# Windowed attention and a SwiGLU block in one kernel: the queries of batch 1 turned by DMA, and all steps in another order

## The chip, the cores and the metric

The kernel runs on one core of a Trainium2 chip. The metric is the device time of one execution in microseconds (us). Engines: PE (TensorE), DVE (VectorE), ACT (ScalarE), POOL (GpSimd), SP (SyncE); SP, ACT and POOL also issue DMA transfers.

## The reference, cut to what matters

```python
q, k, v: (4, 8, 768, 64)            # batch, heads, sequence, head_dim
scores = q @ k.T / sqrt(64)
keep = (key < 8) | (0 <= query - key < 96)       # 8 global keys, a window of 96
scores = where(keep, scores - slope[h] * dist, -1e9)
a = exp(scores - max); a = a / (sum(a) + 1e-9)
x = (a @ v), heads side by side: (3072, 512)
g = x @ w_gate; out = (silu(g) * (x @ w_val)) @ w_out      # 512 -> 1536 -> 512
```

Inputs and output are float32; the kernel works in float16 with float32 sums in PSUM.

## The kernel before, in words

The kernel is one long list of steps, the string `ORDER`, read from left to right by a small interpreter at the end of the kernel. A step is a name and numbers (`g.2.11@4` is the gate product of token tile 2, feature block 11, into PSUM bank 4). Each step issues its instructions to one or more engines; every engine then runs its own instructions strictly in that order and waits only for data, for a buffer or for a bank. So where a step stands in the list sets what stands behind it on its engine. The steps are:

- Loads, all issued by POOL with a cast to float16: `Lh.i.half...` (half a sequence of keys, i=0, or queries, i=1, of some heads of batch 0, line 249), `L4.i.g` (four heads of batch 1 at once, 384 KB, line 287), `Lr.b.i.h` (one head of batch b in rows, 96 KB, line 292), `Lv`, `Lt`, `LG` (values, their tail, the global rows; lines 255, 261, 266), `Lw` (512 columns of the gate or value weights, line 299), `Lo` (output weights, line 307). A load waits until the eighth load before it has landed, since eight semaphores go round.
- Turning keys and queries so that the head dimension lies on partitions. Batch 0: `T` on PE (line 358), then `k` and `q` copies out of PSUM. Batch 1: `U` on PE (line 399), then `kw` (keys) and `qw` (queries, line 412). Batches 2 and 3: `D.b.hp.i`, a DMA transpose that SP issues (line 420) into `kN` (keys, i=0, three buffers) or straight into `qT` (queries, i=1, six buffers); `K.b.hp.e` (lines 427 to 430) spreads the keys `kN` into chunks, with its large copy on the engine e (V is DVE, A is ACT) and two small ones on DVE. hp is a pair of heads.
- Attention: `c.b.g.u` scores on PE (line 448), `x` their exp on ACT (457), `m` the mask on DVE (478), `w.b.half.what` the weighing on PE (505 for the sums, 511 for the values), `i`, `r` the inverse of the sums and its spreading on DVE (521 to 529), `p` the scaled result `xT` on DVE (540).
- The block behind it, for eight tiles of 384 tokens: `g` and `v` products on PE (553), `t` tanh on ACT (559), `s` and `h` the silu and the product on DVE (563, 570), `o.t.i.part` output products on PE (588; 585 for the last rows), `e.t.i` the output's copy on ACT into `osb` (two buffers, line 602) and its store by SP (603). The last rows, `e.7.2`, are copied in halves by ACT and DVE (597, 598) and stored by two queues (599, 600).
- `G` copies the global rows of values along (SP, 283); `fill.n` is n matmuls on ones into a bank that nobody reads (338); `M`, `Z`, `Y`, `VG`, `Gc`, `Li`, `Ld` prepare masks, zeros, first global rows and constants.

Tiles of a kind (`st`, `kN`, `qT`, `osb`, `xT`, ...) share a ring of buffers; a new tile takes the one that was given up first in the order of the program, and its first writer waits for that tile's last reader. `st`, into which keys and queries are loaded, has seven.

The lines that turn batch 1 on PE, and those that turn a batch by DMA:

```python
def tr_whole(bank, hp, i):
    ...
    for j in range(JW):                      # 8 by 2 transposes
        for hi in range(2):
            nc.tensor.transpose(
                t16[64 * hi:64 * hi + 64, PT * j:PT * j + PT],
                stage(1, i, hp // 2)[:, 2 * (hp % 2) + hi, D * j:D * j + D], ident)
...
def tr_dma(b, hp, i):
    ...
    nc.sync.dma_start_transpose(
        out=dst.rearrange("r (t p) -> r t p", t=J),
        in_=stage(b, i, hp // 2)[:, hp % 2].rearrange("p t e d -> p (t e d)"))
```

## Time and profile before

| what | value |
|---|---|
| median of three runs | 245.55 us (245.31 to 247.51) |
| the profiled execution: its time, its span | 247.71 us, 245.6 us |
| PE busy | 234.9 us, 96% of the span |
| DVE, ACT, POOL busy | 162.3, 105.4, 87.0 us |
| L399, transposes of batch 1 on PE | 128, 3.7 us busy |
| L358, transposes of batch 0 on PE | 128, 6.1 us busy |
| DMA queue of POOL, of SP: packets' time as a share of 16 engines' span | 65.2%, 18.5% |

The span runs from the first to the last instruction of the profiled execution; its own time is 2.1 us longer. Busy times of PE overlap, as a matmul starts before the one ahead of it has drained; the spacing of matmuls is read from the chain that ended last, which counts each stretch once. "PEclk" is the share of full clock speed granted to PE, "DMA share" the mean busy share of the 16 DMA engines, over 1 where transfers overlap on one.

### The profile page before, as it was taken

To read this page: it belongs to the slowest core of one execution; us is meant where nothing else is said; L and a number is where in the kernel's file an instruction comes from. 1 tells how busy PE (TensorE), PEld (TensorE's weight loads), DVE (VectorE), ACT (ScalarE), POOL (GpSimd) and SP (SyncE) were. 2 spreads that over 40 slices of the span, in tenths; PEclk is the share of its full clock that TensorE was granted. 3 is DMA by queue.
4 is the path that set the end of the run, shared out by engine and by line. 5 is a ranking of instruction groups with operands and counts; after the bars stand their busy time and mean duration, and the time that the engine had idled before them with its cause. 6 is when DMAs were issued, how large, how long until landed. Compare 5 with 4: busy or idle time off the path is not lost.

```text
span 245.6 us, 7237 instructions
## 1 busy us (share of the span) xinstructions
PE 234.9 (96%) x3112; PEld 137.3 (56%) x3112; DVE 162.3 (66%) x359; ACT 105.4 (43%) x191; POOL 87.0 (35%) x117
## 2 busy tenths in 40 slices
PE   8599999999999999999699999999999999999994
PEld 5376566664554555555355466545555655556643
DVE  5398998785275577837577769834898478505840
ACT  5495733745632533225573253235761142323321
POOL 8698695545999976980000000000000000000000
PEclk9858999999999999999999999999999999999999
DMA  7999999999999999999900374012000300021012
GB/s 103 161 160 161 179 141 178 206 195 91 173 173 144 180 137 160 120 159 200 115 3 0 120 168 42 0 45 88 3 0 15 121 0 3 0 85 43 3 42 86
DMA packets 82095, 24.57 MB, mean 100 GB/s; under 512 B 68896, under 2 KB 79120, under 8 KB 82064
## 3 DMA queue, kind: packets, MB, share of 16 engines
q0 software_dynamic: 64656, 14.20, 65.2%
q1 hardware_dynamic: 17224, 9.77, 18.5%
q8 instruction: 24, 0.39, 0.6%
q10 hardware_dynamic: 184, 0.14, 0.2%
q14 instruction: 7, 0.06, 0.1%
HBM read 28.51 MB, written 6.29 MB: 142 GB/s over the span
## 4 chain that ended last, share of the span: by engine, by line
PE 82%; DMA 9%; DVE 3%; POOL 2%; issue 1%; ACT 1%; ACTq 0%; POOLq 0%
PE PS L553 47%; PE PS L588 25%; PE PS L511 3%; DMA kN<-st 3%; DMA st<-in_q_dram 3%; DMA wv<-in_moe_w_val_dram 3%; PE PS L448 3%; PE PS L505 2%; PE PS L399 1%; PE PS L585 1%; POOL st L249 1%; DVE vS L277 1%; DVE qT L390 1%; ACT th L559 1%; DVE at L478 0%
## 5 line engine op out<-in xcount | busy, mean ns | idle before, releaser
L563 DVE SCALAR_TENSOR_TENSOR sl<-th,PS 128x384 f32<-128x384 f32 x96 | 50.8, 549 | 41.0 <-ACT th L559 40.4
L553 PE MATMUL PS<-xT,wg 128*128 128x384 f16 x384 | 72.6, 326 | 2.2 <-DVE hT L570 2.1
L553 PE MATMUL PS<-xT,wv 128*128 128x384 f16 x384 | 72.2, 326 | 0.1
L559 ACT ACTIVATE th<-PS 128x384 f32<-128x384 f32 x96 | 44.3, 491 | 59.0 <-PE PS L553 50.0
L588 PE MATMUL PS<-wo,hT 128*128 128x512 f16 x276 | 64.6, 379 | 0.0
L570 DVE TENSOR_TENSOR hT<-PS,sl 128x384 f16<-128x384 f32 x96 | 50.9, 552 | 10.4 <-PE PS L553 8.8
L553 PEld LDWEIGHTS <-wg 128*128 128x128 f16 x384 | 36.9, 98 | 28.2 <-issue 2.8
L553 PEld LDWEIGHTS <-wv 128*128 128x128 f16 x384 | 36.7, 98 | 25.6 <-DMA wv<-in_moe_w_val_dram 0.5
L588 PEld LDWEIGHTS <-hT 128*128 128x128 f16 x276 | 26.0, 98 | 28.7
L457 ACT ACTIVATE at<-PS 128x912 f16<-128x912 f32 (+1 forms) x40 | 31.6, 830 | 22.7 <-PE PS L448 22.6
L255 POOL DMA_DIRECT2D vS<-in_v_dram x40 | 33.2, 845 | 8.4 <-DMA wo<-in_moe_w_out_dram 3.0
L602 ACT ACTIVATE osb<-PS 128x512 f32<-128x512 f32 x23 | 13.7, 597 | 41.2 <-PE PS L588 41.2
L478 DVE TENSOR_TENSOR at<-at,masks 128x912 f16<-128x912 f16 (+5 forms) x56 | 22.5, 442 | 1.9 <-ACT at L457 1.9
L540 DVE TENSOR_TENSOR xT<-PS,rb 128x768 f16<-128x768 f32 x16 | 14.6, 952 | 7.2 <-PE PS L511 6.7
L292 POOL DMA_DIRECT2D st<-in_q_dram x16 | 14.4, 915 | 3.1 <-PE PS L553 1.4
L292 POOL DMA_DIRECT2D st<-in_k_dram x16 | 14.2, 912 | 0.5 <-DMA vS<-in_v_dram 0.5
L448 PE MATMUL PS<-qT,kT 64*64 64x152 f16 (+4 forms) x464 | 13.5, 238 | 0.5 <-DVE xT L540 0.4
L448 PEld LDWEIGHTS <-kT 64*64 64x64 f16 x464 | 8.6, 113 | 7.9 <-issue 6.8
L511 PE MATMUL PS<-at,vS 64*32 64x152 f16 (+4 forms) x1024 | 10.5, 218 | 0.4 <-issue 0.4
L511 PEld LDWEIGHTS <-vS 64*32 64x32 f16 x1024 | 9.3, 90 | 2.6 <-issue 2.3
L338 PE MATMUL PS<-ones 128*128 128x256 f16 x44 | 9.1, 387 | 1.2 <-DVE wg L304 1.2
L358 PE MATMUL PS<-ident,st 96*64 96x96 f16 x128 | 6.1, 268 | 3.0 <-DMA st<-in_k_dram 2.6
(50 smaller groups left out, 115.1 us busy)
## 6 DMA issues: line engine op xcount, KB each, us to landing
out_dram<-osb SPq DMA_DIRECT2D x23, 256.0 KB, 3.7
vS<-in_v_dram POOLq DMA_DIRECT2D x24, 91.0 KB, 5.6
wg<-in_moe_w_gate_dram POOLq DMA_DIRECT2D x6, 256.0 KB, 5.7
wv<-in_moe_w_val_dram POOLq DMA_DIRECT2D x6, 256.0 KB, 7.2
wo<-in_moe_w_out_dram POOLq DMA_DIRECT2D x3, 512.0 KB, 14.8
st<-in_q_dram POOLq DMA_DIRECT2D x16, 96.0 KB, 7.2
st<-in_k_dram POOLq DMA_DIRECT2D x16, 96.0 KB, 5.2
st<-in_q_dram POOLq DMA_DIRECT2D x4, 192.0 KB, 7.5
```

The source lines that it names most:

```text
L255: nc.gpsimd.dma_start(out=v_of(b)[CH * c + NG:CH * c + CH, c0:c1, j, :], in_=v[b, h, KC * c0:KC * c1, :].rearrange("(i p) d -> p i d", p=KC))
L292: nc.gpsimd.dma_start(out=stage(b, i, h % 2, True)[:, h // 4, :, h // 2 % 2, :], in_=KQ[i][b, h].rearrange("(t p) d -> p t d", p=128))
L448: nc.tensor.matmul(PS[64 * e:64 * e + 64, bank + hi, col:col + n], lhsT=kT_of(b, hp)[r, CH * c:CH * c + CH], rhs=qTs[b, hp][r, q0:q0 + n], ...
L457: nc.scalar.activation(out=at[:, :, 0:w], in_=PS[:, bank:bank + 2, 0:w], func=AF.Exp, scale=scale)
L478: ENG[e].tensor_mul(a2, a2, m2)
L511: nc.tensor.matmul(PS[r, bank + e, o:o + n], lhsT=V[s, c, j, what - 1::2], rhs=at[s, hi, col:col + n], start=first, stop=last, skip_group_ ...
L540: nc.vector.tensor_mul(x_of(2 * b + half)[:, side::2, :], PS[:, bank:bank + 2, 0:TB], rbs[b, half])
L553: nc.tensor.matmul(PS[:, bank, 0:TB], lhsT=w[:, c, 128 * f:128 * f + 128], rhs=xTs[t][:, c, :], start=(c == 0), stop=(c == NC - 1))
L559: nc.scalar.activation(out=th, in_=PS[:, gv[t, f, 0], 0:TB], func=AF.Tanh, scale=0.5)
L563: nc.vector.scalar_tensor_tensor(out=sl, in0=gv[t, f, "t"], scalar=1.0, in1=PS[:, gv[t, f, 0], 0:TB], op0=AluOp.add, op1=AluOp.mult)
L570: nc.vector.tensor_mul(hTs[t, f // 3][:, f % 3, :], PS[:, gv[t, f, 1], 0:TB], gv[t, f, "s"])
L588: nc.tensor.matmul(PS[:, bank, :], lhsT=lhsT, rhs=wo[:, f, :], start=(f == 0), stop=(f == NFF - 1))
```

## The change

Only the string `ORDER` differs. The steps that are taken out, put in or given to another engine are these; everything else is the same set of steps in a new order.

```
taken out:  L4.1.0 L4.1.1  U.0.1 U.1.1 U.2.1 U.3.1  qw.0.A qw.1.A qw.2.A qw.3.V  and three of eleven fill.4
put in:     Lr.1.1.0 to Lr.1.1.7 (eight)  D.1.0.1 D.1.1.1 D.1.2.1 D.1.3.1
other engine: Li S to A; VG.S.0, VG.A.1 to VG.A.0, VG.S.1; q.1.0, q.3.0 V to A; q.0.1 A to V;
            k.0.0 A to V; k.0.1, k.2.1 V to A; kw.0 V to A; kw.1 A to V;
            K.2.0 V to A; K.2.1, K.2.2 A to V; K.2.3, K.3.3 V to A
```

So the queries of batch 1 are loaded in rows, a head at a time, and turned by DMA transposes; its keys are still loaded four heads at once and turned on PE. The parts of the list of which the text speaks:

```diff
 ORDER = """
-pre Y.0.1.0 Ld.S Y.0.0.0 Lh.1.0.0.2 Z.1 VG.S.0 Z.2 fill.4@0 fill.4@1 fill.4@2 fill.4@3 VG.A.1 Li.S
-fill.4@4 Lh.0.0.2.4 Z.0 M.0 fill.4@5 M.1 Gc.0.0.V Lh.0.0.0.2 T.1.0.1@6 q.1.0.V T.2.0.0@7 T.1.0.0@0
...
-x.0.1.2 L4.1.0 Lv.0.0.0.7 fill.4@3 fill.4@2 Lv.0.7.0.7 Lv.0.3.0.7 m.0.1.0.V fill.4@5 m.0.0.1.V
-w.0.0.0@7 i.0.0 c.0.0.2@0 Lv.0.4.0.7 x.0.0.2 fill.4@6 c.0.0.3@2 x.0.0.3 Lv.0.6.0.7 Lw.0.1.1
...
-p.0.0.0 U.0.1@2 qw.0.A Lw.0.0.1 g.0.7@3 t.0.7 x.0.1.3 g.0.6@0 Lt.0.1 g.0.4@1 g.0.5@6 g.0.3@7
...
-Lr.2.1.1 LG.2.0 w.1.1.1@1 e.2.2 w.1.1.2@6 D.2.1.1 o.2.1.1 Lv.3.1.0.13 o.2.1.2 o.2.1.3 D.3.1.1 r.1.1
-o.2.0.1 p.1.1.0 p.1.1.1 o.2.0.2 o.2.0.3 e.2.1 g.3.6@0 g.3.0@5 e.2.0 g.3.1@1 g.3.2@2 D.2.2.1 Lt.3.0
...
-D.3.0.0 K.2.2.A h.3.3 D.2.3.1 G.2.0 v.3.4@5 G.3.0 Lr.3.0.7 t.3.8 Lv.2.6.0.13 Lr.3.1.0 h.3.1 x.2.0.0
...
-e.7.1 e.7.2 fill.4@3
+pre Y.0.1.0 Ld.S Y.0.0.0 Z.1 Li.A Z.2 VG.A.0 Lh.1.0.2.4 fill.4@0 Z.0 M.2 M.3 fill.4@1 fill.4@2
+Lh.0.0.0.2 fill.4@3 Gc.0.0.V fill.4@4 fill.4@5 Gc.1.0.V T.2.0.1@6 Lh.0.0.2.4 VG.S.1 Gc.0.1.A M.0
+Lh.1.0.0.2 T.3.0.1@7 M.1 Lh.1.1.0.2 T.1.0.0@0 T.0.0.0@1 Lh.0.1.0.2 T.3.0.0@2 q.2.0.V k.1.0.V
+T.2.0.0@3 k.3.0.A T.0.0.1@4 T.1.0.1@5 k.2.0.A q.3.0.A fill.4@0 q.0.0.V q.1.0.A Lv.0.3.0.7 k.0.0.V
+c.0.1.1@2 c.0.1.0@6 x.0.1.1 x.0.1.0 Lv.0.6.0.7 c.0.0.0@4 x.0.0.0 T.1.1.1@0 Lh.1.1.2.4 q.1.1.V
...
+c.0.1.4@3 m.0.1.2.V c.0.1.3@0 fill.4@5 Lw.0.1.1 x.0.1.4 g.0.2@2 x.0.1.3 m.0.1.3.V Lt.0.1 Lv.0.2.7.13
...
+Lr.1.1.6 h.0.5 LG.1.0 s.0.6 Gc.1.1.A w.0.1.1@3 Lr.1.1.2 Lw.1.2.0 Lr.1.1.0 D.1.0.1 w.0.1.2@6 g.0.11@0
...
+v.1.6@7 s.0.4 L4.0.1 L4.0.0 t.1.3 g.1.5@5 g.1.8@2 Lo.1 s.0.8 Lr.1.1.4 G.1.1 D.1.1.1 s.0.11 Lt.1.1
+Lo.0 v.1.3@3 t.1.8 t.1.5 h.0.4 Lr.1.1.7 v.0.11@4 Lo.2 Lt.3.0 s.1.3 v.1.4@0 h.0.11 h.1.3 s.1.5 t.1.4
...
+G.1.0 D.1.2.1 v.1.10@2 o.0.2.2 m.1.0.2.V Lr.2.0.0 h.1.10 o.0.2.3 e.0.2 o.1.1.0@3 c.1.1.0@0 x.1.1.0
...
+h.2.2 Lr.2.1.0 Lr.3.1.6 Lv.2.7.0.13 v.2.1@3 K.2.1.V v.2.6@7 Lr.2.1.3 g.2.7@5 h.2.1 Lr.2.1.4 g.2.6@2
...
+D.2.1.1 o.2.2.2 o.2.2.3 D.2.0.1 c.2.0.1@1 p.1.1.0 g.3.3@4 g.3.5@6 e.2.0 g.3.2@7 e.2.1 LG.3.0 e.2.2
...
+t.3.0 v.3.3@3 h.3.5 Lt.3.1 c.2.1.2@6 Lr.3.1.1 Lv.3.2.0.13 s.3.6 h.3.3 x.2.1.2 s.3.0 m.2.1.2.V Lt.2.0
...
+o.7.0.3 e.7.0 o.7.1.1 o.7.1.2 o.7.1.3 e.7.1
 """
```

The order in which SP issues its transfers is, in the new list: D.1.0.1, G.1.1, D.1.1.1, D.1.3.1, G.1.0, D.1.2.1, six stores (tiles 0 and 1), D.2.0.0, G.3.1, D.2.1.0, D.2.3.0, D.2.2.0, D.2.1.1, D.2.0.1, three stores (tile 2), D.2.2.1, D.3.0.0, D.2.3.1, and so on. In the old one: two stores, G.1.0, G.1.1, four stores, D.2.1.0, D.2.0.0, D.2.3.0, D.2.0.1, G.2.1, a store, D.2.1.1, D.3.1.1, two stores, D.2.2.1, D.2.2.0, D.3.0.0, D.2.3.1, and so on.

## The prediction

> **What bounds the kernel now.** I read the span and the forty slices first, then stretches between chosen moments, then the chain that ended last, then the DMA issues with their landings.

> ```profile
> span 245.6 us, 7237 instructions
> ...
> PE   8599999999999999999699999999999999999994
> ...
> PEclk9858999999999999999999999999999999999999
> DMA  7999999999999999999900374012000300021012
> ```

> PE is the bound: busy in all slices but the first, the twentieth and the last. The DMA engines are full for twenty slices too (to about 120 us), so a change that moves work from PE to DMA moves it onto the second bound.

> ```profile
> core 0: us, PE busy (x) PEld busy (x) DVE busy (x) ACT busy (x) POOL busy (x), PEclk, DMA share, GB/s
> 7.15:10.56 3.41, 0.82 (x28) 0.57 (x24) 1.01 (x3) 1.07 (x3) 1.61 (x3) 1.00 1.32 168
> 10.56:20.80 10.24, 9.65 (x171) 7.31 (x172) 9.02 (x26) 7.24 (x15) 8.78 (x13) 0.50 1.47 157
> 20.80:25.57 4.77, 4.39 (x219) 3.31 (x218) 4.12 (x9) 2.48 (x4) 4.77 (x8) 1.00 1.29 160
> 25.57:111.40 85.83, 85.34 (x1138) 49.01 (x1139) 58.72 (x125) 38.68 (x70) 65.79 (x84) 1.00 1.67 159
> 111.40:124.50 13.10, 10.95 (x112) 5.99 (x110) 8.48 (x21) 7.23 (x13) 0.00 (x0) 1.00 1.10 141
> 124.50:241.90 117.40, 117.40 (x1412) 67.04 (x1412) 76.99 (x159) 44.14 (x83) 0.00 (x0) 1.00 0.15 43
> ```

> The first product starts at 25.57. From there to 241.9 PE is never idle but for 2.15 us in the fifth stretch. The second stretch shows the clock: granted 0.50 although PE is busy 9.65 of 10.24 us, with transposes and scores.

> ```profile
> 45.13 1.99 PE PS L399 x80
> ...
> 48.52 0.46 PE PS L399 x16
> ...
> 54.81 0.46 PE PS L399 x16
> ...
> 111.41 8.12 DMA kN<-st
> 119.53 0.02 issue
> 119.55 0.02 ACT kT L427
> ```

> In the chain, L399 is the transposing of batch 1, and the idle time near 120 is a DMA transpose that took 8.12 us to land. That transfer carried the keys of heads pair 2, batch 2; the copy K.2.2 waited for it on ACT and DVE, and what stood behind it there held PE.

> ```profile
> kN<-st SPq DMA_TRANSPOSE x3
> qT<-st SPq DMA_TRANSPOSE x3, 3.1
> ```

> These are the issues from 125 to 160 us, after the loads have ended: a transpose lands in 3.1. By the trace's completion events, the eleven issued from 83 to 113 us, among the loads, took 7.3 to 9.2, and the one at 116.65, as the loads ran out, 4.5.

> **The change, part by part.** I lay the new order out on a calendar of PE: 0.65 us a product or output step, 0.30 a score step, 0.55 or 0.68 a weighing, 0.46 a transposed group (all from the chain), from a first product at 25.57. The old order ends at 238.4 on it, and did at 241.85; the new one ends at 237.0.

> *PE work removed.* Four groups of 16 transposes: 25 to 29 ns each (1.99/80, 0.46/16), 64 make 1.6 to 1.8. One group stood before the first product, so the stream behind it loses 48: **-1.4** (-1.2 to -1.6). Their evictions (three of 0.80 on ACT, one of 0.95 on DVE) go as well, worth nothing: ACT is busy 43%, DVE 66%.

> *Start.* The fourth load lands at 10.8 in either order, but the new one brings the first half of all keys and queries in its first four. From there: two transposed groups (0.85 at this clock), copies (0.55 and 0.9), scores, three exps (0.9 each) to 15.8, copies of keys 0.6, a fourth exp to 17.3, three masks (0.6 each) to 19.0, where the weighing starts. In the old order that step starts at 21.01, and 4.56 us later the first product: 23.6 now, 2.0 earlier. The eighth value load is the 17th instead of the 19th (the old 17th landed at 20.2), and the weights for the first product come by about 23. But of four fills (16 ones-matmuls) between the first six and the first product only two are left, and it was two or three of the old ones, from 18.48, that stood before the clock rose at 20.80. Transposes and scores alone held 0.50 for 10 us. So the new products start at half pace until 2.3 us (the dense part before 20.80) to 5.7 us (one more period of 3.41) of dense work have gone by, 0.85 of it in the last fill: 1.4 to 4.8 us at half pace, 0.7 to 2.4 lost. I take 1.5, together **-0.5** (-2.0 to +0.9).

> [...]

> *Loads.* Two loads of 384 KB (L287) become eight of 96 KB (L292). Completions follow each other by 1.9 us for the first kind and 0.65 for the second, so 8 x 0.65 - 2 x 1.9 = 1.4 us more. Four more DMA transposes share the engines: 0 to 1.6 us each (in 125 to 160 us the SP queue's packets took 27.2% of 35 us, 9.5 us, for six transposes and three stores). At 0.8, three of them delay the last load of output weights by 2.4, with POOL's issues behind it 3.3 to 3.8 later. POOL's own 113 issues become 119, 0.70 against 0.91 us each. No weight becomes late: Lo.2 by 61 stands against its use at 67 on the calendar.

> *Batch 1's queries.* SP issues D.1.0.1, G, D.1.1.1, D.1.3.1, G, D.1.2.1 and then the stores. D.1.3.1 waits for the 53rd load: as many bytes had landed at 53.4 in the old order, and with 1.4 and two transposes it is about 56 to 57. D.1.2.1 goes at 59.3 to 60.7 and lands, at 4.5 to 7.4, at 64 to 68. Its reader c.1.1.0 stands at 65.0; products and outputs wait behind it on PE. **+0.7** (0 to 3).

> *Batch 2's keys and queries.* Three stores stand ahead of D.2.0.0 on SP, two buffers for three; so D.2.0.0 goes at 82.4 and D.2.1.0 at 84.8, landing 7.8 to 9.2 later (the old D.2.1.0 and D.2.0.0) at 92.6 to 94. K.2.1 stands on DVE at 92.7, with h.2.1 behind it, which frees a bank of PE 2.6 us later: **+0.5** (0 to 2). D.2.2.0 takes K.2.1's buffer, at 95; D.2.1.1 and D.2.0.1 follow on the queue by 1.3 to 2.0 each; D.2.0.1 goes at 98.2 and lands by 105.6 to 107.4, against c.2.0.1 at 106.3: **+0.7** (0 to 2).

> *The next two transposes.* The stores e.2.0, e.2.1, e.2.2 now stand ahead of D.2.2.1, D.3.0.0, D.2.3.1. e.2.2's copy needs e.2.0's buffer: that store goes at 102.5 and lands 3.7 to 6.6 later (stores of 103.02 and 107.50), 106.2 to 109.1. So D.2.2.1 goes at 107.3 to 110.2, D.2.3.1 2.8 later at 110.1 to 113.0, and with the loads still running (to 117 before, about 120 now) lands after 7.4: 117.5 to 120.4. Its reader c.2.1.2 stands at 114.1, or 114.8 behind the wait above. **+3.7** (0, if it takes the 4.5 of 116.65, to 5.6). This replaces the old idle time: **-2.15**.

> *Tail.* The last store is a whole one: copy 0.60 on ACT instead of 0.42, landing 2.0 in both: **+0.2** (0 to 0.5).

> Sum: -1.4 - 0.5 + 0.7 + 0.5 + 0.7 + 3.7 - 2.15 + 0.2 = +1.75, a span of 247.3. The profiled execution took 247.71, 2.1 above its span; the runs' median, 245.55, equals the span. I add the sum to the median: **247.3**.

> **Rivals.** *Slower: the transposes late for three readers.* If transposes among the loads take 9.2 (the top row) and not 7.4, each of the waits at c.1.1.0, c.2.0.1 and c.2.1.2 grows by up to 1.8; the third is met by a PE that has already waited at the second, so two of them add up: +3.6, 250.9. It decides as soon as D.2.3.1 lands after 118. For it: eleven of eleven among loads took 7.3 or more. Against: the loads thin out near 118.

> *Faster: no transpose is waited for.* At 4.5 us or less each of these terms is 0, and -1.4 - 0.5 - 2.15 + 0.2, with 0.6 for small waits, give -3.25: 242.3. For it: D.2.2.0 no longer stands behind stores. Against: the same eleven rows.

> *The clock is up at the first product.* Then the start is -2.0 and the time 245.8. [...] Against it: the row at 0.50; for it: two fills remain, and the 3.41 us window before 10.56 had 1.00 after six fills.

> *The start gains nothing:* a copy or a value load is 2 us late, and the clock needs the whole 5.7: the start is +2.4 and not -0.5, the time 250.2. For it: the tight chain of copies above; against it: DVE and ACT wait for PE and DMA in the old start (idle 1.2 of 10.24 and 3.0 of 10.24 us in the second stretch).

> **How the numbers follow.** Forecast 0.40 (own range 245 to 250); late transposes 0.22; none waited for 0.20; clock up 0.08; start without gain 0.10. One per cent (2.5 us, to 243.1 and 248.0) is about what a measurement of this kernel tells from no change. Faster takes 0.17 of the third, 0.03 of the forecast, 0.03 of the clock's: 0.23. Slower takes 0.22, 0.08 and 0.12 of the forecast: 0.42. The rest, 0.35, is within 1%. Range 241.8 to 252.0: from the case without waits to the late transposes with their bounds.

> **What would show it.** L399's count falls from 128 to 64; the first product starts near 23.6 with 325 ns between products for 1.4 to 4.8 us; POOL's last issue comes near 112 instead of 108.4; a PE wait of 2 to 5 us stands between 113 and 122, ended by a transpose of queries, with small ones at 65 and 107. The prediction is wrong if transposes among the loads land in under 5 us, if PE waits elsewhere (a bank held by DVE), or if the first product is not before 25.

## The result and the profile after

The changed kernel took 255.37, 256.97, 259.48 and 261.22 us, a median of 258.23. Ratio to the kernel before: 1.0403, 95% interval 1.0297 to 1.0508. So it is slower by 4%, about 10 us, where the forecast was 247.3 and the range ended at 252.0. The profiled execution is the longest of the four, 261.22 us with a span of 258.9; the ratio leaves out the two longest, 259.48 and 261.22, which count as slow, so what this profile shows is held against three faster ones below.

The page of the changed kernel, its span and three of the forty-slice rows:

```profile
span 258.9 us, 7103 instructions
...
PE   7499999996799999979199999989999989999994
...
PEclk9856999999799999999769999999999999999999
DMA  7999999999999999999950544012000210011003
```

PE shows dents in the tenth and eleventh slice, in the eighteenth, and a hole in the twentieth. The clock row dips behind the first dent and behind the hole: not foreseen. The loads last longer: POOL's last issue comes at 118.8 us, not 108.4.

The same stretches as before, cut at PE's waits (us, then busy time and count of each engine, then granted clock, DMA share, GB/s):

```profile
core 0: us, PE busy (x) PEld busy (x) DVE busy (x) ACT busy (x) POOL busy (x), PEclk, DMA share, GB/s
...
62.67:65.36 2.69, 0.25 (x2) 0.10 (x2) 0.02 (x1) 0.00 (x0) 1.36 (x2) 1.00 3.34 78
...
112.48:114.65 2.17, 0.26 (x3) 0.11 (x2) 0.00 (x0) 0.60 (x1) 2.17 (x3) 1.00 1.64 201
...
122.70:128.40 5.70, 0.24 (x2) 0.15 (x2) 1.69 (x4) 0.28 (x1) 0.00 (x0) 0.86 1.83 154
128.40:133.30 4.90, 4.90 (x39) 2.38 (x42) 1.82 (x3) 2.24 (x3) 0.00 (x0) 0.50 1.14 93
```

Three stretches in which PE does almost nothing, and a fourth in which it is busy all the time at half clock. The chain of work that ended last says what was waited for (start, us, what):

```profile
61.70 9.51 DMA qT<-st
...
112.74 1.91 issue
...
117.56 10.79 DMA qT<-st
...
171.95 0.87 issue
...
211.37 0.74 issue
```

The first and third are DMA transposes of queries: D.1.2.1 (issued at 61.70, landed at 71.2) and D.2.3.1 (117.56 to 128.4). The rows called issue are time in which PE waited for nothing that the profile shows. The one at 112.74 stands at c.2.0.1, after two of its twelve products. All twelve read the same tiles of queries and keys, and the last transpose among them, D.2.0.1, had landed at 108.4.

So there are two suspects, the transposes (theory A in the expectations below) and these issue waits, and a third: that the order itself, by its queue of stores and its banks, loses the time (theory B).

### The profile page after: what moved, and what is told of

Same layout as the page of the kernel before. It is cut to its first block, busy times and chain, and to the rows that moved or that the text cites. A ratio compares the mean times of both kernels' runs of the same rounds, so it can differ in the third digit from the quotient of the medians.

```text
span 258.9 us, 7103 instructions
## 1 busy us (share of the span) xinstructions
PE 235.9 (91%) x3036; PEld 136.8 (53%) x3036; DVE 161.8 (63%) x352; ACT 105.1 (41%) x194; POOL 92.2 (36%) x123
## 4 chain that ended last, share of the span: by engine, by line
PE 66%; DMA 22%; POOL 8%; issue 3%; ACT 0%; SPq 0%; POOLq 0%
PE PS L553 36%; PE PS L588 22%; DMA qT<-st 8%; DMA wo<-in_moe_w_out_dram 6%; DMA wg<-in_moe_w_gate_dram 3%; PE PS L448 3%; DMA st<-in_k_dram 3%; PE PS L511 3%; DMA wv<-in_moe_w_val_dram 2%; POOL vS L255 2%; POOL st L292 2%; PE PS L505 1%; PE PS L585 1%; POOL wg L299 1%; POOL st L249 1%
## 5 line engine op out<-in xcount | busy, mean ns | idle before, releaser
L559 ACT ACTIVATE th<-PS 128x384 f32<-128x384 f32 x96 | 45.3, 491 | 58.2 <-PE PS L553 49.3
L588 PE MATMUL PS<-wo,hT 128*128 128x512 f16 x276 | 64.7, 382 | 0.4 <-DMA wo<-in_moe_w_out_dram 0.4
L570 DVE TENSOR_TENSOR hT<-PS,sl 128x384 f16<-128x384 f32 x96 | 51.4, 553 | 14.4 <-PE PS L553 12.3
L588 PEld LDWEIGHTS <-hT 128*128 128x128 f16 x276 | 26.6, 99 | 30.5 <-issue 1.2
L478 DVE TENSOR_TENSOR at<-at,masks 128x912 f16<-128x912 f16 (+5 forms) x56 | 22.6, 443 | 23.7 <-ACT at L457 23.6
L602 ACT ACTIVATE osb<-PS 128x512 f32<-128x512 f32 x23 | 13.7, 597 | 50.6 <-PE PS L588 47.9
L448 PE MATMUL PS<-qT,kT 64*64 64x152 f16 (+4 forms) x464 | 15.3, 259 | 10.8 <-DMA qT<-st 8.9
L292 POOL DMA_DIRECT2D st<-in_q_dram x24 | 20.6, 867 | 3.9 <-DMA vS<-in_v_dram 3.4
L448 PEld LDWEIGHTS <-kT 64*64 64x64 f16 x464 | 10.1, 126 | 19.0 <-issue 16.7
L292 POOL DMA_DIRECT2D st<-in_k_dram x16 | 13.8, 880 | 1.6 <-DMA vS<-in_v_dram 1.1
L511 PE MATMUL PS<-at,vS 64*32 64x152 f16 (+4 forms) x1024 | 11.1, 227 | 1.6 <-issue 1.6
L511 PEld LDWEIGHTS <-vS 64*32 64x32 f16 x1024 | 9.8, 94 | 3.5 <-issue 3.1
L521 DVE STREAM_TRANSPOSE dT<-PS 128x384 f32<-128x384 f32 x8 | 4.6, 581 | 6.4 <-PE PS L505 5.8
```

Source lines behind the costliest of these rows:

```text
L292: nc.gpsimd.dma_start(out=stage(b, i, h % 2, True)[:, h // 4, :, h // 2 % 2, :], in_=KQ[i][b, h].rearrange("(t p) d -> p t d", p=128))
L448: nc.tensor.matmul(PS[64 * e:64 * e + 64, bank + hi, col:col + n], lhsT=kT_of(b, hp)[r, CH * c:CH * c + CH], rhs=qTs[b, hp][r, q0:q0 + n], ...
L478: ENG[e].tensor_mul(a2, a2, m2)
L511: nc.tensor.matmul(PS[r, bank + e, o:o + n], lhsT=V[s, c, j, what - 1::2], rhs=at[s, hi, col:col + n], start=first, stop=last, skip_group_ ...
L559: nc.scalar.activation(out=th, in_=PS[:, gv[t, f, 0], 0:TB], func=AF.Tanh, scale=0.5)
L570: nc.vector.tensor_mul(hTs[t, f // 3][:, f % 3, :], PS[:, gv[t, f, 1], 0:TB], gv[t, f, "s"])
```

## The experiments

**Repeats.** Four kernels were meant to undo one part each, but their edits of the order were not in the files: e1, e3 and e4 ran the changed kernel's order once more (e3 with an unused function) and e2 the kernel before. What was expected of them is on record:

> The new order of steps, with batch 1's queries loaded as two whole loads and transposed by PE again. Theory A (the four extra DMA transposes are late among the loads and delay the loads): the PE waits of 2.44 us before c.1.0.1 and 0.97 us before c.1.1.0 go, POOL's last issue comes at 109 to 112 us instead of 118.9, PE gets 1.6 us of transposes back, the wait before c.2.1.2 shrinks since the loads end earlier, but does not go: 247 to 251 us. Rival B (the order of all steps itself is what costs the time, by its queue of stores and transposes for batch 2 and by banks): 254 to 257 us. Rival C (eight loads of rows cost the loads more than the transposes do): like A, this run does not tell A from C.

> The old order of steps, with only batch 1's queries changed to eight loads of rows and four DMA transposes, at the place of the second whole load. Theory A: POOL's last issue moves from 108.4 to 116 to 118 us, the readers of the weights and of batch 2's rows wait; 250 to 255 us. Rival B: as before the change or 1 us less, 244 to 247 us.

> The changed kernel with the four DMA transposes of batch 1's queries replaced by four copies on ACT; the turning of these queries is left out, the eight loads of rows stay. Theory A: POOL's last issue at 110 to 112 us instead of 118.9, no PE wait at c.1.0.1 or c.1.1.0 over 0.5 us, a shorter wait at c.2.1.2: 247 to 251 us. Rival C (the eight loads of rows themselves delay the loads): the last issue stays at 116 or later, the time above 252 us. Rival B: 254 us or more.

> The changed kernel with D.2.2.1, D.2.3.1 and D.3.0.0 moved on SP's queue ahead of the three stores e.2, directly behind D.2.0.1; nothing else. If the wait of 5.45 us before c.2.1.2 comes from this place in the queue, it falls to 0 to 1 us, and with it the second stretch of 6.8 us at a clock of 0.50 behind it goes (2.4 us of PE time): 249 to 252 us. If the transposes land late wherever they stand (theory A in its strong form, the engines being full), the wait only shrinks by 2 to 3 us: 253 to 255 us.

They decide nothing between the theories, but they are repeats. The changed order gave ratios of 1.0336 (1.0271 to 1.0400), 1.0394 (1.0323 to 1.0465) and 1.0426 (1.0351 to 1.0502), so 1.039 as the mean of four with the first measurement. The kernel before gave 1.0009 (0.9973 to 1.0046). Their profiles show what is steady (all in us; first product, then PE's waits):

| profile, span | first product | c.1.0.1 and c.1.1.0 | c.2.0.1 (issue) | c.2.1.2 | later issue waits |
|---|---|---|---|---|---|
| changed, 258.9 | 24.73 | 3.4 | 1.9 | 5.5 | 0.9, 0.7 |
| e1, 252.0 | 21.82 | 4.1 | 2.6 | 1.3 | 0.8, 0.8 |
| e3, 253.8 | 22.92 | 4.3 | 2.4 | none | 1.3, 0.8 |
| e4, 253.4 | 22.53 | 3.2 | 2.6 | 1.6 | 0.9, 1.0 |

The waits for batch 1's queries and at c.2.0.1 are in all four; the one at c.2.1.2 is none to 1.6 us in the three faster executions, and 5.5 us only in the longest. In the second profile of the kernel before (span 244.2) this is PE's longest wait:

```profile
PE PS L511 <- issue: 0.8, 1, 0.8
```

So the 2.1 us near 118 us, which the prediction took off as a gain, are in one profile of the kernel before and not in the other.

**Back to PE in the new order (f1).**

```diff
- Lr.1.1.0 ... Lr.1.1.7, D.1.0.1, D.1.1.1, D.1.2.1, D.1.3.1
+ L4.1.0, L4.1.1 in place of Lr.1.1.5, Lr.1.1.6
+ U.0.1@5 qw.0.A behind s.1.5; U.1.1@2 qw.1.A behind s.1.8
+ U.2.1@0 qw.2.A behind h.1.8; U.3.1@6 qw.3.V behind h.0.8
```

> The new order of steps, but batch 1's queries loaded as two whole loads and turned by PE again (four groups of 16 transposes, put behind s.1.5, s.1.8, h.1.8 and h.0.8); the rows' loads and the four DMA transposes of them are gone. Theory A (these four transposes are late among the loads and hold PE at c.1.0.1 and c.1.1.0, and the clock falls behind that wait): 4 us of waits and 1.7 us of half clock go, 1.6 us of transposes come back, POOL's last issue comes at 108 to 111 us instead of 114 to 119: 250 to 252.5 us. Theory B (the order itself costs the time, at c.2.0.1, c.2.1.2 and by the loading of PE's code): 254 to 257 us.

Measured: 254.71 us median, ratio 1.0309 (1.0240 to 1.0379), inside theory B's span; POOL's last issue at 108.2. Two rows of PE's waits in f1:

```profile
PE PS L511 <- issue: 2.3, 2, 1.3
PE PS L399 <- DVE sl L563: 1.7, 2, 0.9
```

The waits for batch 1's queries are gone and the loads end as early as before. But the four groups that I put in find their banks held by DVE (the second row, and another 1.3 us for L570: 3.0 in all), and issue waits remain, in other places: 0.99 us at 109.7 and 1.33 at 136.6, none at c.2.0.1. PE has 128 instructions more in front of c.2.0.1 (64 transposes and their weight loads). That pointed to the program's place, not to data.

**Rows and transposes in the old order (f2).**

```diff
- L4.1.0, L4.1.1, U.0.1, U.1.1, U.2.1, U.3.1 and their copies qw
+ Lr.1.1.0 Lr.1.1.2 D.1.0.1 Lr.1.1.4 Lr.1.1.6 D.1.1.1 Lr.1.1.1 Lr.1.1.3
+ D.1.2.1 Lr.1.1.5 Lr.1.1.7 D.1.3.1      (at the place of L4.1.1)
```

> The old order of steps, with only batch 1's queries changed: eight loads of rows and four DMA transposes at the place of the second whole load, no transposes of queries on PE. Theory A: POOL's last issue moves from 106 to 108 us to 113 to 117 us, readers of weights or of batch 2's rows wait for more than the 1.6 us that PE is spared: 248 to 254 us. Theory B: the transposes are hidden, 243 to 246 us.

Measured: 256.41 us median, ratio 1.0400 (1.0310 to 1.0491), above both spans; POOL's last issue at 116.0. The two longest waits of PE (this kernel's lines stand one further down than before's):

```profile
PE PS L400 <- DMA st<-in_k_dram: 5.3, 1, 5.3
PE PS L554 <- DVE hT L571: 2.6, 1, 2.6
```

In the old order the rows and transposes cost as much as the whole change, though not in the same places. Batch 1's keys, loaded behind them, are 5.3 us late for PE's own transposes (L399 before), and 6.8 us at a clock of 0.50 begin within that wait. The second row stands at the product at which the kernel before lost its 2.1 us. Issue waits of 0.6 and 1.5 us are in this profile too. Theory A holds here, where the transposes stand ahead of loads that are needed soon.

**No transposes in the new order (f3).** The turning of batch 1's queries is left out.

```diff
- D.1.0.1, D.1.1.1, D.1.2.1, D.1.3.1
+ DC.0 ahead of o.0.0.0; DC.1 behind o.0.2.0; DC.2 DC.3 ahead of G.1.0
+ def copy_rows(hp): nc.scalar.copy(out=q_of(1, hp)..., in_=stage(1, 1, hp // 2)...)
```

> The changed kernel with the four DMA transposes of batch 1's queries replaced by four copies on ACT, so that the turning of these queries is left out; the eight loads of rows stay. Theory A: no wait over 0.5 us at c.1.0.1 and c.1.1.0, no half clock behind it, POOL's last issue 110 to 112 us: 248 to 251 us. Theory C (the small packets of the eight loads of rows delay the loads, not the transposes): the last issue stays at 114 or later, 252 to 255 us. Theory B: 254 to 257 us.

Measured: 252.80 us median, ratio 1.0230 (1.0147 to 1.0312). The median lies in the span of theory C (that the loads of rows are what delays the others), but its sign is missing: the eight loads of rows are still there, yet POOL's last issue comes at 108.3, as with two whole loads in f1. So theory C falls, and the 1.4 us that I had priced for the rows are nothing. From 40 to 110 us the hardware queue (SP's stores and transposes) took these shares of the 16 engines (packets, MB, share), in f3 and, in the second fence, in the changed kernel:

```profile
q1 hardware_dynamic: 6176, 3.38, 23.7%
```

```profile
q1 hardware_dynamic: 9200, 3.70, 34.1%
```

10.4% of 70 us is 7.3 us of all engines for four transposes of batch 1, and f3's window holds one later transpose and two stores more in exchange: an estimate of 1.8 us each at the least. By POOL's last issue, 113.0 to 118.8 in seven profiles of the new order with them against 108.3, it is 1.2 to 2.6 each. The prediction had 0.8.

What is left in f3 is the issue wait. PE's timeline there (lines stand five further down: L516 is L511, L593 is L588, L453 is L448), and the code's queue in 106.5 to 108 us:

```profile
103.41 1.36 PE L516 MATMUL PS<-at,vS 64*32 64x48 f16 x144
104.70 1.47 PE L593 MATMUL PS<-wo,hT 128*128 128x512 f16 x6
106.10 0.25 PE L453 MATMUL PS<-qT,kT 64*64 64x152 f16 x2
109.20 0.39 PE L453 MATMUL PS<-qT,kT 64*64 64x152 f16 x10 [2.85 <-issue]
```

```profile
q8 instruction: 1, 0.02, 4.0%
```

The trace has 23 packets of 16,384 bytes on this queue for 6,082 recorded PE instructions (products, weight loads and a few of the sequencer's), one for 264. In the changed kernel, its repeats, f3 and f5, the wait stands at the 3,010th recorded PE instruction, and the later ones at the 4,289th and 5,569th: 1,279 and 1,280 apart, five times 256 within one; g4's waits below stand 511 and 2,304 apart, two and nine times 256 within one. So 256 recorded instructions to a packet, a block in what follows, are an estimate from these distances. The instructions from 2,754 to 3,010 are nearly all weighing products and their weight loads (239 of a run of 288 that takes 1.4 us), then six output products; PE is through them 2.9 us after it began. The next packet is on its way from 106.8 to 107.7, and PE goes on at 109.2, 1.5 us after its end. That is theory D: a packet that holds only short instructions is used up before the next one has come.

Behind this block the wait is 1.9 us in the changed kernel, 2.4 to 2.6 in its repeats, 2.85 in f3 and 3.8 in f5.

**Transposes earlier, and SP's queue changed (f5).**

```diff
+ Lr.1.1.4 Lr.1.1.7 D.1.0.1 D.1.2.1 D.1.1.1 D.1.3.1 ahead of L4.0.1 (taken from their places)
+ D.2.2.1 D.2.3.1 D.3.0.0 behind D.2.0.1, ahead of e.2.0, e.2.1, e.2.2
```

> The changed kernel with its eight loads of rows together ahead of L4.0.1 and the four transposes of them issued there, some 10 to 17 us earlier, and with D.2.2.1, D.2.3.1, D.3.0.0 ahead of the three stores e.2 on SP's queue. Theory A: no wait at c.1.0.1, c.1.1.0 and c.2.1.2, one or two stretches of half clock gone; the wait of 1.9 to 2.6 us at c.2.0.1 stays: 248 to 251 us. If the transposes are as costly to the loads wherever they stand, the weights behind them become late instead (waits for wo or for batch 1's keys at 50 to 65 us) and it is 253 to 257 us.

Measured: 254.99 us median, ratio 1.0380 (1.0309 to 1.0451). In its profile the waits at c.1.0.1, c.1.1.0 and c.2.1.2 are gone, as expected, but POOL's last issue stays at 117.3, and the longest wait is larger than in any other profile of this order:

```profile
PE PS L448 <- issue: 3.8, 1, 3.8
```

A wait of 2.5 us for a load of weights behind the first product comes on top, and no gain can be told from the intervals. The expected 248 to 251 was wrong.

**Weighings spread (g1).**

```diff
- w.1.1.2@1 w.1.1.1@6          + w.1.1.2@1 o.2.1.1 o.2.1.2 o.2.1.3 w.1.1.1@6
- w.2.1.0 w.2.1.1 w.2.1.2      + w.2.1.0 o.4.2.1 o.4.2.2 w.2.1.1 o.4.2.3 o.4.1.0 w.2.1.2
- w.3.0.2 w.3.0.1              + w.3.0.2 v.5.6 o.5.1.0 o.5.1.1 w.3.0.1
```

> The changed kernel with three weighing steps moved, so that output steps stand between two weighings of one half: w.1.1.2 ahead of o.2.1.1; w.2.1.1 behind o.4.2.2 and w.2.1.2 behind o.4.1.0; w.3.0.1 behind o.5.1.1. Theory D (PE's code comes in packets of 16 KB for 256 instructions; where one packet's instructions are all short weighing products, PE is through before the next packet is there): the waits that the profile calls issue, 1.9 to 2.6 us at c.2.0.1 and 0.7 to 1.3 us at 165 to 172 and at 204 to 211 us, fall to under 1, 0.5 and 0.5 us, with the half clock that sometimes follows the first: 3 to 5 us faster than the changed kernel, 250 to 252.5 us. Rival (the wait at c.2.0.1 is for data, a bank or a transpose whose event the profile lacks): it stays 1.9 us or more, 254 to 256 us.

Measured: 251.44 us median, ratio 1.0232 (1.0177 to 1.0288), inside theory D's span. PE's timeline, with the same work as in f3's:

```profile
106.86 0.73 PE L511 MATMUL PS<-at,vS 64*32 64x48 f16 x72
107.52 2.12 PE L588 MATMUL PS<-wo,hT 128*128 128x512 f16 x9
109.57 0.73 PE L511 MATMUL PS<-at,vS 64*32 64x48 f16 x72
110.23 1.47 PE L588 MATMUL PS<-wo,hT 128*128 128x512 f16 x6
111.63 0.54 PE L448 MATMUL PS<-qT,kT 64*64 64x152 f16 x12
```

All twelve products of c.2.0.1 run in one piece. Of the issue waits one of 0.6 us is left, at 201, behind a run of weighings that was not broken up. By itself this run does not rule out a bank: DVE's copy that frees this step's banks starts at 107.7 us here and at 110.6 in the changed kernel. But in f3 that copy had ended at 105.2, before the first two of the twelve products ran, so no bank held the other ten; and the next run leaves the order alone.

**Only the program's place moved (g4).**

```diff
+ 64 products of 8 columns on bank 7, behind M.3, in PE's idle time at the start
```

> The changed kernel, same order, with 64 products of 8 columns (and their 64 weight loads) put into PE's idle time before the first loads have landed: nothing moves but the place of every later PE instruction, by 128, in the program. Theory D: the wait at c.2.0.1 goes or falls under 0.8 us, since the packet that was all weighing now holds output steps too; shorter waits called issue may come up elsewhere: 251.5 to 255 us. Rival (data): the wait at c.2.0.1 stays at 1.9 us or more, 254 to 256.5 us.

Measured: 258.37 us median (255.30 to 259.72), against 255.37 to 261.22 of the changed kernel: no gain. But the wait at c.2.0.1 is gone, and in the chain others stand elsewhere:

```profile
23.26 2.19 issue
...
41.46 3.35 issue
...
142.07 1.68 issue
```

They stand at the 962nd, 1,473rd and 3,777th recorded instruction, within one or two of 3,010 less eight and six, and plus three, times 256. (A wait of 2.6 us at c.2.1.2 is put to a transpose.) The place decides which step waits, as theory D says, and the rival of data or a bank falls. My expectation of less time was wrong: the shift moved such waits and did not remove them.

The packets of the changed kernel's trace make theory D sharper. Five blocks of 256 take under 3 us there. Three end in a wait, and PE goes on 1.3 us after the end of a packet (113.35, 171.50 and 210.86 us) in each. Two, of 2.3 and 2.1 us, end at the 2,242nd and 5,058th instruction without a wait: a packet had started 3.3 and 1.0 us before PE entered them, and not, as at the waits, between 0.3 us before and 2.5 us after. In the kernel before, a block of 1.4 us loses only 0.4 us at the 3,010th instruction: its packet ended at 102.8, and PE goes on 1.4 us later. So a short block alone is not enough; what makes a packet start early or late is not known.

**Both causes taken away (g2).** The turning of batch 1's queries is left out.

```diff
 f3's edit (D.1.0.1, D.1.1.1, D.1.2.1, D.1.3.1 out, four copies in) and g1's (w.1.1.2, w.2.1.1, w.2.1.2, w.3.0.1 moved)
```

> The four transposes of batch 1's queries replaced by copies (the turning is left out) and the three weighing steps moved, both together. If late transposes (5 us in the run without them) and the code's packets (4.5 us of waits and 1.7 us of half clock in that run's profile) are all that the new order loses, 243 to 247 us, the level of the kernel before or below; if there is a third cause, 249 us or more.

Measured: 246.98 us median, ratio 1.0028 (0.9990 to 1.0065). From the mean of 1.039, f3's edit takes 1.6%, g1's 1.6% and both 3.6%: of about 9.6 us, about 3.9 are the transposes, about 3.9 the code's packets with what follows them (by the intervals each is known to some 2 us), and the two together explain 8.9. PE's two longest rows of waits in g2:

```profile
PE PS L453 <- DMA qT<-st: 1.8, 2, 1.2
PE PS L516 <- issue: 1.0, 1, 1.0
```

The first is c.2.1.2, the second a run of weighings that was not broken up. They use up most of what the earlier first product (24.21) and the spared transposes give, so a third cause of any size is not seen.

**The new start with the old rest (g3, g5, g6).** Batch 1's queries are turned by PE in all three. g3:

```diff
+ the new order's steps up to x.0.1.4, its loads of weights in the old order's sequence
+ behind them all other steps in the old order; L4.1.0 ahead of L4.1.1, LG.2.1 behind Lo.2,
+ U.0.1@1 qw.0.A ahead of v.0.8
```

> The new order up to its first product (with the old order of weights' loads), then the old order of all other steps, batch 1's queries turned by PE as before. The new order's first product stands at 22.2 to 24.7 us against 25.6 to 26.4 us of the old one. If the start is worth what it shows, 241 to 244 us; if the loads put off to get it make weights or batch 1's keys late, 245 to 249 us.

Measured: 245.53 us median, ratio 1.0001 (0.9972 to 1.0029). Its first product stands at 22.47, but this follows:

```profile
24.68 1.62 PE L553 MATMUL PS<-xT,wg 128*128 128x384 f16 x9 [1.40 <-ACT at L457]
```

ACT had the first product's tanh ahead of an exp that frees this product's bank. And a code packet cost 1.17 us at 103. So two edits:

```diff
+ x.0.1.3 ahead of g.0.7; g.0.5 g.0.3 ahead of g.0.6
+ w.1.1.2@6 behind o.2.1.2 (g5)
+ D.2.2.0 behind D.2.1.1 on SP's queue as well (g6)
```

> The new start with the old rest, and two edits: x.0.1.3 ahead of the first product, so that ACT no longer waits for the first product before that exp, with g.0.5 and g.0.3 ahead of g.0.6; and w.1.1.2 behind o.2.1.2, so that three output steps stand between the weighings. If the start's gain was only used up by the waits of 1.4 us (ACT) and 1.2 us (code), both go: 242.8 to 244.3 us, a ratio of 0.989 to 0.995. If the start gives nothing, since weights or keys come later by as much: 245 to 246 us.

> The same with D.2.2.0 moved on SP's queue directly behind D.2.1.1, ahead of two stores and of D.2.2.1. In one of two profiles of the old order the copy of these keys was 2.1 us late for PE near 118 us, in the other not at all: 0 to 1 us less than the run without this move, 242 to 244.3 us; if the stores behind it hold up output buffers instead, up to 1 us more.

Measured: g5 244.64 us median, ratio 0.9983 (0.9958 to 1.0009); g6 244.63, ratio 0.9976 (0.9954 to 0.9999). In g5's profile the packet's wait at 103 is gone; waits for loads stand in its place, 0.8 us at 25 and 0.4 to 0.5 at 28 and 44. Both gained less than expected. g6 is the fastest kernel here, by a quarter of a per cent, hardly to be told from no change.

## Why the prediction was wrong

Two steps failed. The price of a DMA transpose among loads was too small, for its reader and for the loads behind it: taking batch 1's four transposes away gives back about 3.9 us. And waits for PE's own code had no term in the sum at all: breaking up the runs of weighings gives back about 3.9 us as well.

*The sign of the first mechanism was right, its size was not.* That transposes among the loads come late for three readers was foreseen. The table shows two of these, c.1.1.0 in every profile and c.2.1.2 in three of four. A fourth reader was not named: c.1.0.1 waits 0.9 to 3.2 us for D.1.1.1, which could not be issued before 54 to 57 us, as a load of its rows took some 13.5 us to land among the loads of weights. The prediction counts eleven transposes of the old order between 83 and 113 us at 7.3 to 9.2; the trace has nine, and in the second profile of that order, where the loads ended some 2.5 us earlier, the last three of them took 3.7 to 4.7.

*PE work removed, -1.4:* about right. L399 counts 64 and not 128. From first product to last, without waits, PE took 213.0 us in g2's profile and 214.3 and 213.7 in the two of before.

*Start, -0.5 (-2.0 to +0.9):* the first product was 0.8 to 4.4 us earlier (21.82 to 24.73 against 25.57 and 26.20), and the clock was 1.00 at or within half a microsecond of it: the rival "the clock is up" was right on the clock. The last stretch at 0.50 before the first product lasted 3.4 to 13.7 us in these profiles. Put ahead of the old order the new start was worth next to nothing: 0 in g3, and 0.4 us, inside the interval, in g5. In most profiles waits of 0.5 to 2.5 us for weights or a bank stand behind the earlier first product; in e4's there is none above 0.2 us before 55 us, and its first product stands 3.0 to 3.7 us earlier, beyond the forecast's bound of 2.0.

*Loads:* the mis-sized term. The rows cost 0 and not 1.4; the four transposes 1.2 to 2.6 us each of the loads' time, and not 0.8. "No weight becomes late" did not hold: PE waits 0.4 to 1.3 us for output weights in three of the four profiles.

*Batch 1's queries, +0.7 (0 to 3):* measured 3.2 to 4.3 us at c.1.0.1 and c.1.1.0, above the upper bound. D.1.2.1 was issued at 61.7, 1.0 us after the forecast's latest, and took 9.5 us to land. I had priced it by 4.5 to 7.4, the first a row from when the loads were running out; the rows of 7.3 to 9.2 were the ones from among the loads.

*Batch 2:* no wait at K.2.1 (+0.5 forecast). c.2.0.1 did wait, 1.9 to 2.6 us (+0.7 forecast), but for code, not for D.2.0.1. *The next two transposes, +3.7 (0 to 5.6):* 5.5, 1.3, none and 1.6; inside the bounds, mostly at their lower end.

*The old idle time, -2.15:* should not have been in the sum. The wait is in one of two profiles of before, the one whose execution took 247.71; I added the sum to a median of runs that had most likely paid nothing there.

*Not in the sum at all:* code packets (3.5 to 4.5 us with the later two waits), and the clock, which in these profiles dropped to 0.50 for 3.4 or 6.8 us at most waits of about 2.5 us or more; by estimate up to 1.7 us are lost for each 3.4 (half of it, at 0.50).

The sum with measured sizes, e1's profile (252.0) against the second of before (244.2): start -4.4, PE work -1.4 as forecast, PE's waits 11.9 instead of 1.0, so +10.9, one stretch of 3.4 us at half clock +1.7, tail +0.3: +7.1 of the 7.8 us between them.

## What to carry to other kernels

Price a DMA transpose that runs beside loads by rows from among the loads, once for its reader's wait (8.6 to 11.6 us from issue to landing for batch 1's queries here) and once for what it takes from the loads behind it (about 2 us each here). Count PE's instructions between long ones: a run of some 250 short products and weight loads was at times followed by a wait that no semaphore explains (0.7 to 3.8 us here, and none behind two of five such runs in the changed kernel), and three output steps put between them took it away at c.2.0.1 (1.9 to 2.6 us in the changed kernel and its repeats, none in g1). And before a wait in a profile is booked as a gain, see whether a second profile has it.

## What the runs showed of the hardware beyond what was expected

The profile counts PE's code on the same 16 DMA engines as the loads (4.0% of them for 1.5 us while one packet came in f3). In the changed kernel single packets took 0.9 to 1.4 us after the loads had ended, and up to 2.8 us (at 117.7) among loads and transposes. Whether the wait would shrink on idle engines was not tried: the waits of 0.7 to 1.3 us at 160 to 211 us, with the loads over, are shorter than the 1.9 to 3.8 us among them, but other instructions stand there, and the kernel before lost only 0.4 and 0.8 us among its loads.
